# Four PSUM evictions per batch cut to one bank each in a fused recurrence and FFT-convolution kernel

## The chip, the cores and the metric

The kernel runs on one core of a Trainium2 chip. The metric is device time in microseconds; 459.4 us is the median of three runs of the kernel before (458.79 to 459.71). Engines are TensorE (PE; its weight loads are shown apart as PEld), VectorE (DVE), ScalarE (ACT), GpSimd (POOL) and SyncE (SP, which issues all transfers).

## The reference

For 4 batches of 6272 steps and 256 channels, a gated recurrence feeds a long circular convolution with two multiplicative gates:

```python
f = lower_bound + (1 - lower_bound) * sigmoid(f_logit)
h[t] = f[t] * h[t-1] + (1 - f[t]) * x[t]           # scan over 6272 steps
x1, x2, x3 = split(h @ w_proj, 3)
conv = irfft(rfft(x2, axis=1) * rfft(filter_fft, axis=0))
out = (x1 * conv * x3) @ w_out
```

## The kernel before

The DFT of length 6272 is done as 49 x 128: a first DFT over one factor, then one over the other (FT), the product with the filter's spectrum, and the two inverses. All of it is matrix products with tables that the kernel computes at the start.

The work is cut into *operations* (`op`, L80): a kind, the engines that may do it, a function that emits its instructions, and tags that it reads and writes. An operation of TensorE takes one or two of the eight PSUM banks (`take`); its result is evicted by an operation with `src` set to it. The operations are emitted in the order of a table, ORDER (L128): each entry is three characters that hold the number of the operation, its engine and its first bank. So the order on every engine, the choice between ScalarE and VectorE for each eviction (`either`, L305), and the banks are fixed by this table, and each engine works through its own list in order, waiting at semaphores.

The kinds, with the lines that the profile shows:

- **Start**: the filter is loaded, rotated (`rot`, evicted as `f2`), transformed (FF1, L661, evicted as `afs`; FF2, L679, evicted as `hw`), and its spectrum stored in DRAM and loaded back in units (Hu, Hx).
- **Recurrence of a batch** (`hgrn`): loads of x and f_logit, sigmoid on ScalarE (L337), product on GpSimd (L339), transposes on TensorE (`su`, L351), the gate f on ScalarE or VectorE (L364, L366), the scan on VectorE (L372), into HA. The recurrence of batch b+1 is worked between the steps of batch b.
- **x2 projection** (`phase_p`): 49 rows of 256 columns, two matmuls each (L725), four rows to an operation of two banks, five in the last of 12; evicted as `x2` into X.
- **First DFT** (`phase_f1`, F1, L737): 16 units of eight matmuls, two banks, evicted as `A` into HA (1024 columns). It reads all of x2.
- **Second DFT and product** (`unit`, F2, L795): the product with the spectrum is either one VectorE instruction from PSUM (L816, shown as PP) or a ScalarE copy followed by a GpSimd product (L825).
- **Inverse over q** (I2, L835): per unit 16 matmuls in two banks, evicted as `Th` (784 columns).
- **Gates** (`gate`, x13, L400): x1 and x3 per chunk, one bank each; x1 is copied out (`xs`), x3 either copied out and multiplied on GpSimd (L431), or multiplied on VectorE from PSUM (L422), into zt.
- **Output** (`phase_o`): the second inverse (I1, L869) reads all of Th; VectorE multiplies it with zt (`y`, L875); output projection (L887), four rows in two banks; evicted as `o` into one of eight places, which are then stored.

Evictions go through helpers, so ScalarE's show as L291 or L293 and VectorE's as L296 or L298, told apart by the tile that they write: X is x2, HA with 128 x 1024 is A, HA with 98 x 512 the copy ahead of a GpSimd product, Th is Th, osb, PP or HA in f32 is o, gx is a gate.

Of the kernel before, what the change touches and what calls it, by code (L numbers as in the profile page):

```python
# [21 lines left out]
S = 6272  # L22
# [26 lines left out]
NX2 = 12  # L49
# [15 lines left out]
class Plan:  # L65
# [63 lines left out]
    "AAYA+gBFgAMYABIAgVACIBBgAvWBMgAeUBTgAxSAdVBIgAkWBPgA9YANIAmUAoWA/TBGRBADBCYBogBDTBWgAtVAPIBNVAOABagBEDADgBdgBHBBhg"  # L129
    "BUTBJYBkgBOFDwgBQYBKQD8gBVDAcSArXATYAyVASIBRWDxgAVYBXAAsSApSBLIBSGBYUEIgBbSARIBZED9gEJgBeIAQAAUIBfQAFgBiVBgABpYAWY"  # L130
    "BcCEUgBlIBmQBjFAaTBnIAhXEVgBqTAZSBrDAqSAlWBwWBuSBxODyAB3UB1QBvKD+AAuWB4MBzWByYDzYB2IB+SB0GAbVB/KB6QCAUEKAB7ID0SB5Y"
    "AEYCFWD1CCBMD/YD4QCGGD2KCHUEggD5AEhgCDWCIED6IEASCEGELYCKUEBKEEWCLEECKCOQEsgEFGEtgAiUCCYCVUCJYAXYCPAEGOCXSEWAEMQCYK"
    "EQWAIAEXYAHACQSE4gEROCWEE5gCRKENAAfUAwUESOEiACTSCSYEYUCUCEOIEcWEjYFCgEdGCeSEZMFDgAKACgQEeOCfCChACZYCaSEuAEaMEkWCnQ"
    "CbCEvYElOClUE6ACoICdgAjSEmOEoQCmECjSFMgAJACiYEwUE7YEpIFNgCkCCwWB9gEqIExEE0SCxGEyMFWgCqQE1CBsYFXgC1WCrAE2KE8UFEACpY"
    "E/QBtYC2OC3SFggFAAE9MFFYCuWFhgC4CETgFBICvGAnTAGgFOACzWD7gE+MFGSCyYC0GFPYFJQFHKC+UFqgFKAFIKFrgC6WC/EC7GFQUC5YCNgFLI"
    "AYYDASFYADHWFRMFTQCMgDBCFZYFSMDIGDFSFUADQWDGCF0gDDUFVIFiAB8gDKSCcgDCYDJYDEMEnYEPgFaQDRGDLCFjYDXWFbIDVUF1gALADOSDYO"
    "DWEFcIDPCFdWDMgD3YFsADTUMTgDSYFeOFkQDUEFtYDgSFfOFlACtgFnUDhCFmIDeWFoEDaSDZYDfGErYFpMFuQF2ADbCDlWGigFvIDnUDmGF+gMfg"
    "DjSDNgF3YFwIDoEFxWC9gEbYDkCC8gJQVFyODiYDpYG0gDqQE3YJSFFzOJRTEHYDrAJVUDdgEzYJWSJTrJXEDtgF4WF7QF5GJUYEDYJYqDuUF/gF8I"
    "JaTJZYEfYDvEF6OJbSF9ICsgJfXJcLGUQJhHDsgMVAGQWGVIMggGSTGRGGGQDcgGTDGMWGHIGIUGNGJdqGCQGJEJeYGESGDIGKUGFCGOQGLEGAWGPI"
    "MhAGrgGWTGBGMUgG9gJgSGXDMrgJkRJiqMsgJlXJpQJjYJnHGYSJrIJmBGeWGZKJqUJoYGfGGaQJuVJssGbAGjWJtYGcSGnuJwFJvRGdCJzUJxpJ0Q"  # L140
    "GoYJ1EJ4XJyYJ2IGgSGsUJ6HGhKJ3YG1QGwEGluJ5XG5AHGSGkYJ7vGxYGmYJ9VHQgHHCJ+RGusJ8YGpWJ/FHMSGvYGqGG3oGtYHZgG+UG6YKABHIW"
    "HNKG4YGyQHJGHAsHKSGzAG2YHigG/YG7WKBYHLCHCsHBYKCQG8GHOTHRRHDYHrgHPLKDVHTBKEIHSYKHTMtAHVpHUYHEQKIXKJDKFtHWYKMWHFAKKv"
    "HaSKGYKOGMuYH+gH0UKLYHeqHXWH1EH4QHcqHfYHYGHjUHkYHbYH5AHnsHdYIHgH2WMiYHgSH3GHlsHoYHsQHhCH6WHuoHmYIQgHpUMWYH7GH/SHwo"
    "HvYHqEH8WKNQIBCIIUH9OHxYIZgIDqHtYIRRICYIKEHyWITBKPoIEYKRTHzGIMsKQYKSUIiQIAYKTDIsgILYIFWIjAINYKUsKWTIVpKVYKXVIGGMXQ"
    "KZFIJYI1gKYLIUYIWYIaWMYAMbUIeGMZIIOSM3gMcEKbXISYIPCMdMIbYIXQKaYKdHImSIYAIcuMegMjUM4gInCIkQMkMIdYIfYIoWIlAKcTMlMKgS"
    "JHgIpGItQKerKiCIqUMnWIvoKfYIxAKhTNDgMoGIyYIgRIrMNEgIwYM5AMpOI+gKlQI2UIhBKjrMvWIuYKnAM6YI6sKkYMzSMwGKmQNQgI4EMxOKqR"
    "I7YNPgM0CIzUKsBI5YM1KM7WI0ENFAKrVKooKvSKttKpYM8GM/QJAYI3YKuYNGYKxCJIUM9ONbgNAAI8SNcgJMEMqgNBIKwWJKEK0XI9CI/UKyuK2H"
    "K1QJDsKzYJLYK5WK3ANHSNRAJBsK4YNLQNICNmgK7ONSYJEYJCYJFUNlgNMANJKK6WJGEK+XNdANNIK/VNTTJJYLAHNeYK8uNXQNUDLBtK9YLDXNvg"
    "NYANVLLEWLCYNwgLFHLISLJVLKCLNXLGuLLFNfSNZILHYJNYLPHNiVNgCLOXN6gNnANhKLMYN5gJOQNjFNoYLQvRtTJPANkNLRYRuXRvDLSQRwHLXS"
    "LTINxANpUNsWLYKNqENyYLUQODgNtGOEgNrMLZSLVANuOLcUMaYLaCLWgNzQLdMRyXN0ALhSR0HN1IN2UN7ALmWONgN3ELiKOOgLeQN8YLbgOFAN4M"  # L150
# [24 lines left out]
    "ZjEbZYZrubaRZZYaBgbbSdkgbfQbdCZpuZsYZaUbcBbhAd5SbeYZbMZqYZkQZwWeVgd6CZlIeWgaCUZ0Gd7KZoYUqgbgQZxYaGEZ1YUlgbkXaEEblR"
    "ZyubiAZtUbmHZ5SZzYZuEbnpbjYeBWZ7qboYZ9CeFQeCGZ+YbpUeggdsAZ8YZ2SeDObrEbqVZ3CbuUeEgbstbvWZ6YeGAaHYefgbwMbzXbtYeXAeNS"
    "eHIb0Vb1Hb4UbxueOCeIgaFYZ/Qb2tbyYb6Eb5WePKb3YaAAeRUb9XepgaDYeSEb7ueYYaIQeqgb/HeTMb8Yb+WaJAcCXcDTcAucEHcHVUtQcFreUY"
    "cBYcJFcISUuId8YehAcGYcMWcKqeZQcLYcNOecUeiYeaAinSezgedEebIioTe0gcOWiqDeeMipCcRQcPGejScSIcWUcQgekCemWerAcXMA2Qe9gcTQ"
    "e+genGesYelKcYUcUAeoOcbScZEcVgcgQUvgccKetWe1AewUchIcdSe2YfHgexEfIgeuGeyMcagAzRceCclQevOe/AA0Vd4Ye3Ue6ScmIfAYe4EciW"
    "fSge7CfRge5McnQcjGe8KcqUcoAA1XcvWcrMfJAfBQfEScwOfCAfKYisVfFCitUfDIcsWivEiuFfGKc0QeQYctGfLUdgYc1IcugcxSfMEfTAfNMfUY"  # L180
    "c5QcyCfOWc6IczgfVUfPGc2ScfgfWEckgfQOc7Qc3CfXMfYWc4gdDUfZOc8Ac+SfaOdEMfdWftQc/KfeGffUfuIfnSfgEfbWfoKfvQfcOfjUfwAdAS"
    "fkEfhWdBCfrQfiGdCgcpgfxSfsAdIWfyCfpQdJOirYflVfqAixTiwYfmFiyUizLi2Xi0EdKQfzSi4HdLIi1Yf1Uf0Cf3Qf2Mf5Wf4Af9Si3Uf6GgBq"
    "A3Ri7Vi5EgFWf/qgCYi9Ff7QgNTi6YgJGi8Vf8IgAYgngjAXi+tf+YjBSgGYjCHgKYgDQi/YgPDjDqjFXgEAgRrjEYgVSjGVgQYgXCgHujKQgSYjHH"
    "gdRjMAjLUjItgIYgwggeBgLWjNsjJYgOYg5gjPQgMGgZqjOYgYYgfUjQRggEgjWjRIgaYghSjSBjUUgWYhCggkOgiCjVVgTQjWEjXNglSgoWgUAgmK"
# [12 lines left out]
def kernel(  # L197
# [72 lines left out]
    def At(u):  # L270

        return [("At", u % NA)]
# [438 lines left out]
    def phase_p(b):  # L711
        hn = [("hn", kh, c) for kh in range(2) for c in range(NCHK)]
        for g in range(NX2):
# [4 lines left out]
            def rows(pb, nb=nb):  # L718
                return PS[:, pb:pb + nb].rearrange("m a (r e) -> m (a r) e", e=256)
# [258 lines left out]
```

## Time and profile before

| | before |
|---|---|
| median of three runs | 459.4 us |
| span of the profiled execution | 458.7 us |
| instructions | 14602 |
| busy: PE, DVE, ACT, POOL | 444.4, 406.4, 400.5, 301.9 us |
| granted TensorE clock | 1.000 |
| HBM over the span | 257 GB/s |

The page gives the profiled execution by its span, from the first to the last instruction; the 0.7 us to the median of the runs lie around it or are the difference between executions. Busy times are the union of an engine's records. A record of ScalarE or VectorE ends when its last write is through, which overlaps the start of the next one by about a tenth of a microsecond; a matmul's end is modelled. In a line of a timeline the first number is the start, the second the length, and "xN" says that N instructions were merged into it; in brackets stands the idle time ahead of it and what ended it. In a line of groups the numbers after the bar are busy time and the mean of one in ns. In a line of waits: total, times, longest.

### The profile page before, as it was taken

Reading aid. Unit: us, or ns where it says so; the run is one execution under the profiler, and the core shown is the slowest. Engines: PE = TensorE matmul, PEld = TensorE weight load, DVE = VectorE, ACT = ScalarE, POOL = GpSimd, SP = SyncE. Lnnn points to the kernel's source line nnn. Section 1 sums busy time; section 2 is a strip of 40 time slices with the busy share of each in tenths; the row PEclk is TensorE's granted clock in tenths of the full one; section 3 lists DMA queues with packets and bytes.
Section 4 is the critical chain, followed back from the end, with each engine's and each line's share of the span. In section 5 each row is a group of like instructions: output and inputs, shape, how many; then the busy total and the mean of one; then the engine's idle time right before and its main releaser. Section 6 shows DMA issues by size and latency. Waiting matters only on the chain.

```text
span 458.7 us, 14602 instructions
## 1 busy us (share of the span) xinstructions
PE 444.4 (97%) x6009; PEld 346.8 (76%) x6009; DVE 406.4 (89%) x459; ACT 400.5 (87%) x551; POOL 301.9 (66%) x279
## 2 busy tenths in 40 slices
PE   8998999999999999999999999999999999999996
PEld 6777777867766889777668879767768798777785
DVE  8389998699999997999999986999999984999974
ACT  4899998999999988989998969999999869889563
POOL 5377993179899742988996525979896503878500
PEclk9999999999999999999999999999999999999999
DMA  8998999957898898368869897388789542576077
GB/s 321 384 374 300 339 402 372 334 149 210 253 334 273 287 302 325 122 195 298 289 236 317 311 309 298 139 300 282 232 318 307 188 186 93 184 227 201 34 285 292
DMA packets 45298, 121.53 MB, mean 265 GB/s; under 512 B 4400, under 2 KB 8496, under 8 KB 45232
## 3 DMA queue, kind: packets, MB, share of 16 engines
q1 hardware_dynamic: 45232, 120.60, 74.8%
q8 instruction: 47, 0.77, 0.7%
q14 instruction: 19, 0.16, 0.1%
HBM read 86.12 MB, written 31.98 MB: 257 GB/s over the span
## 4 chain that ended last, share of the span: by engine, by line
PE 64%; DVE 12%; ACT 8%; DMA 7%; issue 5%; POOL 2%; SPq 1%; DVEq 0%; ACTq 0%; POOLq 0%
PE PS L400 15%; PE PS L725 9%; PE PS L835 9%; PE PS L351 6%; PE PS L887 6%; PE PS L795 6%; PE PS L737 6%; DVE HA L372 5%; DMA X<-in_moe_filter_fft_dram 4%; DVE ys L875 3%; PE PS L661 3%; DMA XT<-in_x_dram 2%; PE PS L869 2%; ACT fTs L364 2%; DMA out_dram<-PP 2%
## 5 line engine op out<-in xcount | busy, mean ns | idle before, releaser
L339 POOL TENSOR_TENSOR XT<-XT,FL 128x1024 f32<-128x1024 f32 (+1 forms) x49 | 109.7, 2243 | 53.9 <-ACT FL L337 47.3
L372 DVE TENSOR_TENSOR_SCAN HA<-fTs,HA,PS 128x512 f16<-128x512 f32 (+1 forms) x96 | 113.2, 1204 | 1.8 <-ACT fTs L364 1.0
L400 PE MATMUL PS<-HA,W 128*128 128x490 f16 (+1 forms) x416 | 102.9, 368 | 1.7 <-issue 0.7
L825 POOL TENSOR_TENSOR PP<-HA,Hu 98x1008 f16<-98x1008 f16 x40 | 83.9, 2104 | 8.0 <-ACT HA L291 3.9
L291 ACT CAST HA<-PS 128x1024 f16<-128x1024 f32 (+1 forms) x98 | 79.1, 834 | 5.3 <-PE PS L737 2.7
L431 POOL TENSOR_TENSOR zt<-gx 128x490 f16<-128x490 f32 (+1 forms) x37 | 44.9, 1219 | 43.0 <-issue 15.6
L875 DVE TENSOR_TENSOR ys<-PS,zt 128x1024 fp32r<-128x1024 f32 (+1 forms) x52 | 58.7, 1152 | 10.0 <-PE PS L869 7.0
L816 DVE TENSOR_TENSOR PP<-PS,Hu 98x1008 f16<-98x1008 f32 x56 | 65.8, 1202 | 0.9 <-issue 0.5
L364 ACT ACTIVATE fTs<-PS,cc 128x512 f32<-128x512 f32 (+1 forms) x85 | 56.1, 675 | 5.8 <-PE PS L351 4.8
L887 PE MATMUL PS<-Wo,ys 128*128 128x256 f32 x392 | 58.1, 294 | 1.6 <-DVE ys L875 1.3
L400 PEld LDWEIGHTS <-W 128*128 128x128 f16 x416 | 34.8, 97 | 31.6 <-issue 8.1
L835 PEld LDWEIGHTS <-PP 98*128 98x128 f16 x1024 | 50.0, 97 | 10.8 <-issue 1.8
L835 PE MATMUL PS<-VV,PP 98*128 98x98 f16 x1024 | 55.9, 206 | 0.7 <-DVE PP L816 0.5
L887 PEld LDWEIGHTS PS<-Wo,ys 128*128 128x128 f32 x392 | 49.8, 189 | 6.4 <-DVE ys L875 1.4
L291 ACT CAST Th<-PS 128x784 f16<-128x784 f32 x59 | 48.3, 821 | 5.7 <-PE PS L835 5.2
L293 ACT ACTIVATE gx<-PS 128x490 f32<-128x490 f32 (+1 forms) x86 | 49.7, 585 | 2.4 <-PE PS L400 1.0
L337 ACT ACTIVATE FL<-FL 128x1024 f32<-128x1024 f32 (+1 forms) x49 | 49.2, 1009 | 0.0
L422 DVE TENSOR_TENSOR zt<-PS,gx 128x490 f16<-128x490 f32 (+1 forms) x67 | 42.8, 650 | 2.7 <-PE PS L400 1.2
L725 PE MATMUL PS<-W,HA 128*128 128x256 f16 x392 | 44.6, 273 | 0.2
L725 PEld LDWEIGHTS <-HA 128*128 128x128 f16 x392 | 43.0, 142 | 1.2 <-issue 0.2
L351 PE MATMUL PS<-iden,FL 64*128 64x64 f32 x736 | 41.9, 230 | 1.1 <-DVE Hx L296 0.5
L351 PEld LDWEIGHTS PS<-iden,FL 64*128 64x128 f32 x736 | 31.3, 138 | 14.3 <-DVE HA L372 2.6
(129 smaller groups left out, 738.6 us busy)
## 6 DMA issues: line engine op xcount, KB each, us to landing
FL<-in_f_logit_dram SPq DMA_DIRECT2D x45, 512.0 KB, 5.6
XT<-in_x_dram SPq DMA_DIRECT2D x45, 512.0 KB, 6.2
Hu<-H SPq DMA_DIRECT2D x39, 512.0 KB, 4.7
out_dram<-osb SPq DMA_DIRECT2D x22, 512.0 KB, 4.4
out_dram<-PP SPq DMA_DIRECT2D x16, 512.0 KB, 5.2
Hx<-H SPq DMA_DIRECT2D x13, 512.0 KB, 4.5
out_dram<-HA SPq DMA_DIRECT2D x10, 512.0 KB, 4.9
X<-in_moe_filter_fft_dram SPq DMA_DIRECT2D x9, 512.0 KB, 7.3
```

The source lines that it names most:

```text
L291: nc.scalar.copy(dst, src)
L339: op("u", {"POOL": 0.1 + 0.553 * nb}, lambda e, xt=xt, ft=ft: nc.gpsimd.tensor_tensor(xt, xt, ft, op=AOP.mult), r=[("ft", k)], w=[("xt", k)])
L351: nc.tensor.transpose(bank(pb)[:, at[p] + j:at[p] + hn:nb], src[ps, j, cols], iden[ps, ps])
L364: nc.scalar.activation(fT, sT, AF.Identity, scale=by, bias=1.0)
L372: nc.vector.tensor_tensor_scan(h, fT, bank(pb)[:, 512 - hn:512 + hn], init, op0=AOP.mult, op1=AOP.add),
L400: nc.tensor.matmul(PS[:, p, 0:n], W13[:, kh, js], HA[:, HB[kh] + t0:HB[kh] + t0 + n], start=(kh == 0), stop=(kh == 1))
L725: nc.tensor.matmul(pp[:, r - r0, :], column(HB[kh], q_of(r)), W2[:, kh, :], start=(kh == 0), stop=(kh == 1))
L816: nc.vector.tensor_tensor(pr, px.unsqueeze(1).broadcast_to([TB, 2, UE, 63]), hh, op=AOP.mult)
L825: nc.gpsimd.tensor_tensor(pr, spec[:, o, :, 1:64].unsqueeze(1).broadcast_to([TB, 2, UE, 63]), hh, op=AOP.mult)
L835: nc.tensor.matmul(PS[:, ib + o, pr * TB:(pr + 1) * TB], PP[:TB, k, o, n, 2 * pr:2 * pr + 2, :], v[:TB], start=(n == 0), stop=(n == 1))
L875: nc.vector.tensor_tensor(late["ys"][:, yk, :, 0:rn * 128], PS[:, cb:cb + 2, 0:rn * 128], late["zt"][:].rearrange("p k r m -> p k (r m)") ...
L887: nc.tensor.matmul(po[:, i, :], late["ys"][:, yk, kh, i * 128:(i + 1) * 128], Wo[:, kh, :], start=(kh == 0), stop=(kh == 1))
```

## The change

The operations P (x2 projection), F1, I2 and proj are cut into operations of one PSUM bank, each with its own eviction. P becomes 25 operations of two rows (the last of one), NX2 goes from 12 to 25. F1 becomes two operations of four matmuls per unit, with a tag At per half. I2 becomes one operation per half spectrum o, so it waits for the products of that half alone. The output projection becomes one operation for two rows; the store still waits for both halves, and is as large as before. The second inverse I1, `y`, F2, the gates and the recurrence keep their operations. The matmuls are the same in number and shape.

The order table is new as a whole: 2866 operations instead of 2410. On ScalarE there are 737 instead of 548, on VectorE 468 instead of 426. Evictions on ScalarE and VectorE: x2 30 and 18 before, 56 and 44 after; A 55 and 9, then 113 and 15; Th 59 and 5, then 111 and 17; o 49 and 3, then 96 and 4. Gate f on ScalarE and VectorE: 85 and 19, then 88 and 16. The x3 gates done as one VectorE product: 67, then 78. Spectrum products on VectorE: 83, then 84.

```diff
-NX2 = 12
+NX2 = 25
...
-        return [("At", u % NA)]
+        return [("At", u % NA, o) for o in range(2)]
...
+            r0 = 2 * g
+            rn = min(2, Q - r0)
...
-            pp = op("P", {"PE": 0.005 + 0.214 * rn}, mm, r=hn + Wr(0) + Wr(1) + ["W2"], take=nb)
+            pp = op("P", {"PE": 0.005 + 0.214 * rn}, mm, r=hn + Wr(0) + Wr(1) + ["W2"], take=1)
...
-        f1 = op("F1", {"PE": 0.056 * UE}, mm, r=[("x2", g) for g in range(NX2)] + ["D1"], take=2)
...
-        op("A", either(1024), lambda e, pb: copy(
...
+        for h in range(2):
...
+            f1 = op("F1", {"PE": 0.028 * UE}, mm, r=[("x2", g) for g in range(NX2)] + ["D1"], take=1)
+            op("A", either(512), lambda e, pb, k=k + h * UE // 2: copy(
...
-        i2 = op("I2", {"PE": 0.695}, inv,
-                r=[("P", k, 0), ("P", k, 1), ("Pz", k, 0), ("Pz", k, 1), "VA", "VB"], take=2)
-        op("Th", either(784), lambda e, ib: copy(
...
+            i2 = op("I2", {"PE": 0.3475}, inv, r=[("P", k, o), ("Pz", k, o), "VA", "VB"], take=1)
+            op("Th", either(392), lambda e, ib, o=o: copy(
...
-            po = op("proj", {"PE": 0.259 * rn}, proj, r=[("y", yk)], take=2)
...
-            op("o", either(256 * rn), lambda e, ob, place=place, rn=rn: copy(
...
+            for h in range((rn + 1) // 2):
+                hn = min(2, rn - 2 * h)
...
+                po = op("proj", {"PE": 0.259 * hn}, proj, r=[("y", yk)], take=1)
+                op("o", either(256 * hn), lambda e, ob, place=place, h=h, hn=hn: copy(
```

More of the change, by code (lines that the diff above doesn't have):

```diff
@@ L134 @@
[L134 to L138, printed above, removed]
@@ L189 @@
[L189 to L192 removed]
+    "AAYABIAMYACIANIAOAAtRAjXAsWBFgAPIAdXAZWAxWArRAbWAiVBTgBBgA+gBIgBMgBPgA9YBCYATYAVYASIAUIARIBGSAqUBUUAgWA/WAmQBDQBag"
@@ L487, in prepare @@
         op("W", {"ACT": 0.5}, lambda e: act.copy(Wo[:], wo[:]), r=[("W", 0, 0)], w=["Wo"])
-        scr, st = HA[:, A0:A0 + AW], [("At", i) for i in range(NA)]
+        scr, st = HA[:, A0:A0 + AW], [t for i in range(NA) for t in At(i)]
         ti = scr[:, 0:2004].bitcast(I32)
@@ L713, in phase_p, with mm @@
         for g in range(NX2):
-            r0 = 4 * g
-            rn = Q - r0 if g == NX2 - 1 else 4
-            nb = (rn + 1) // 2
-            def rows(pb, nb=nb):
-                return PS[:, pb:pb + nb].rearrange("m a (r e) -> m (a r) e", e=256)
-            def mm(e, pb, r0=r0, rn=rn, rows=rows):
-                pp = rows(pb)
-                for r in range(r0, r0 + rn):
+            r0 = 2 * g
+            rn = min(2, Q - r0)
+            def mm(e, pb, r0=r0, rn=rn):
+                for i in range(rn):
@@ L724, in mm @@
                     for kh in range(2):
-                        nc.tensor.matmul(pp[:, r - r0, :], column(HB[kh], q_of(r)), W2[:, kh, :],
+                        nc.tensor.matmul(PS[:, pb, 256 * i:256 * i + 256], column(HB[kh], q_of(r0 + i)), W2[:, kh, :],
                                          start=(kh == 0), stop=(kh == 1))
-            pp = op("P", {"PE": 0.005 + 0.214 * rn}, mm, r=hn + Wr(0) + Wr(1) + ["W2"], take=nb)
-            op("x2", either(256 * rn), lambda e, pb, r0=r0, rn=rn, rows=rows: copy(
+            pp = op("P", {"PE": 0.005 + 0.214 * rn}, mm, r=hn + Wr(0) + Wr(1) + ["W2"], take=1)
@@ L729, in phase_p @@
+            op("x2", either(256 * rn), lambda e, pb, r0=r0, rn=rn: copy(
                 e, both(xv[:, :, r0:r0 + rn]),
-                rows(pb)[:, 0:rn, :].rearrange("m r (i e) -> m i e r", e=2)), w=[("x2", g)], src=pp)
+                PS[:, pb, 0:256 * rn].rearrange("m (r i e) -> m i e r", r=rn, e=2)), w=[("x2", g)], src=pp)
     def phase_f1(b, u):
-        def mm(e, pb):
-            pa = PS[:, pb:pb + 2].rearrange("m a (i c) -> m (a i) c", c=128)
-            for i in range(UE):
-                j = (u * UE + i) * PW
-                nc.tensor.matmul(pa[:, i, :], X2[:, j:j + 128], D1[:], start=True, stop=True)
@@ L738, in phase_f1, with mm @@
-        f1 = op("F1", {"PE": 0.056 * UE}, mm, r=[("x2", g) for g in range(NX2)] + ["D1"], take=2)
-        k = u % NA * UE
-        op("A", either(1024), lambda e, pb: copy(
-            e, A[:, k:k + UE],
-            PS[:, pb:pb + 2].rearrange("p a (i r k) -> p (a i) r k", r=2, k=64)),
-           w=At(u) + Ax(u), src=f1)
+        k = u % NA * UE
+        for h in range(2):
+            def mm(e, pb, h=h):
+                for i in range(UE // 2):
+                    j = (u * UE + h * UE // 2 + i) * PW
+                    nc.tensor.matmul(PS[:, pb, 128 * i:128 * i + 128], X2[:, j:j + 128], D1[:], start=True, stop=True)
+            f1 = op("F1", {"PE": 0.028 * UE}, mm, r=[("x2", g) for g in range(NX2)] + ["D1"], take=1)
+            op("A", either(512), lambda e, pb, k=k + h * UE // 2: copy(
+                e, A[:, k:k + UE // 2],
+                PS[:, pb].rearrange("p (i r k) -> p i r k", r=2, k=64)),
+               w=[At(u)[h], Ax(u)[h]], src=f1)
@@ L871, in inv @@
                                              start=(rr == 0), stop=(rr == 1))
-            i1 = op("I1", {"PE": 0.115 * rn}, inv, r=[("Th", u) for u in range(NU)] + ["ID"], take=2)
+            i1 = op("I1", {"PE": 0.115 * rn}, inv, r=[("Th", u, o) for u in range(NU) for o in range(2)] + ["ID"], take=2)
             yk = g % 2
```

172 lines of the change are left out of this document (94 added, 78 removed).

## The prediction

> **What bounds the kernel now.** I read the page's busy shares first, then busy time by stretches that I cut around the projection of x2, then the waits of VectorE, then the timelines at the cuts.
>
> ```profile
> span 458.7 us, 14602 instructions
> PE 444.4 (97%) x6009; PEld 346.8 (76%) x6009; DVE 406.4 (89%) x459; ACT 400.5 (87%) x551; POOL 301.9 (66%) x279
> ```
>
> TensorE at 97% looks like the bound. But a matmul's record contains the time in which it drains, so short pauses between groups of matmuls vanish in it. The stretches say more.
>
> ```profile
> core 0: us, PE busy (x) PEld busy (x) DVE busy (x) ACT busy (x) POOL busy (x), PEclk, DMA share, GB/s
> 0.00:30.00 30.00, 27.63 (x171) 21.59 (x173) 18.73 (x51) 21.88 (x23) 15.27 (x35) 1.00 0.94 365
> 30.00:75.50 45.50, 43.57 (x566) 33.43 (x565) 44.29 (x48) 44.30 (x65) 38.10 (x43) 1.00 0.96 345
> 75.50:91.00 15.50, 15.49 (x149) 13.49 (x148) 8.99 (x11) 13.65 (x17) 1.23 (x1) 1.00 0.97 359
> 91.00:171.00 80.00, 77.48 (x1221) 58.10 (x1218) 78.69 (x83) 75.12 (x110) 64.94 (x52) 1.00 0.80 257
> 171.00:187.00 16.00, 16.00 (x170) 15.08 (x169) 12.56 (x12) 12.45 (x14) 6.60 (x3) 1.00 0.73 291
> 187.00:272.00 85.00, 83.81 (x1279) 63.14 (x1278) 82.85 (x87) 78.20 (x116) 65.70 (x54) 1.00 0.78 259
> 272.00:287.00 15.00, 14.93 (x148) 14.16 (x147) 9.84 (x10) 13.38 (x14) 6.52 (x4) 1.00 0.77 310
> 287.00:371.00 84.00, 82.28 (x1276) 61.88 (x1275) 82.03 (x87) 77.29 (x115) 65.00 (x53) 1.00 0.74 253
> 371.00:386.00 15.00, 15.00 (x147) 13.94 (x142) 7.42 (x9) 11.69 (x14) 3.10 (x3) 1.00 0.37 143
> 386.00:430.00 44.00, 43.98 (x582) 31.02 (x580) 41.92 (x50) 38.40 (x57) 33.63 (x34) 1.00 0.51 160
> 430.00:458.70 28.70, 24.25 (x338) 20.96 (x334) 19.07 (x19) 14.14 (x15) 1.78 (x2) 1.00 0.61 244
> ```
>
> There are two kinds of stretch. In four **turns** (75.5 to 91, 171 to 187, 272 to 287, 371 to 386: 61.5 us) TensorE is full and VectorE idles 22.7 us. In the **middles** (91 to 171, 187 to 272, 287 to 371, 386 to 430: 293 us) VectorE idles only 7.5 us, ScalarE 24.0. So the middles last as long as VectorE's work, with ScalarE close behind; the turns as long as TensorE's.
>
> **What a split costs.** Every matmul stays as it is; the evictions of x2, A, Th and o are cut in two. A record's tail overlaps its successor, so the price of an instruction is the spacing in a chain: the chain's length less one record, divided by the others.
>
> ```profile
> 186.94 1.93 ACT L291 CAST HA<-PS 128x1024 f16<-128x1024 f32 x2
> 206.26 1.52 ACT L291 CAST Th<-PS 128x784 f16<-128x784 f32 x2
> 210.58 1.57 ACT L291 CAST HA<-PS 98x512 f16<-98x512 f32 x3
> 280.16 3.49 DVE L296 CAST X<-PS 128x1024 f16<-128x1024 f32 x3 [0.45 <-PE PS L725]
> 62.48 0.68 DVE L296 CAST Hx<-PS 128x512 fp32r<-128x512 f32 x1
> 63.08 1.27 DVE L372 TENSOR_TENSOR_SCAN HA<-fTs,HA,PS 128x512 f16<-128x512 f32 x1
> ```
>
> ```profile
> L291 ACT CAST HA<-PS 128x1024 f16<-128x1024 f32 x55 | 55.1, 1025 | 3.9 <-PE PS L737 2.7 <-POOL PP L825 0.5 <-issue 0.2
> L291 ACT CAST HA<-PS 98x512 f16<-98x512 f32 x43 | 24.0, 590 | 1.3 <-PE PS L795 0.9
> L296 DVE CAST X<-PS 128x1024 f16<-128x1024 f32 x18 | 21.6, 1222 | 11.8 <-PE PS L725 11.8
> L296 DVE CAST Th<-PS 128x784 f16<-128x784 f32 x5 | 4.9, 970 | 0.0
> ```
>
> ScalarE: 1024 columns 0.91 us (1.93 - 1.02), 784 about 0.70, 512 0.49 ((1.57 - 0.59) / 2). VectorE: 1024 1.13, 512 0.60 (63.08 - 62.48), 784 0.88 (its 0.97 less the 0.09 by which 1.22 exceeds 1.13). Either way a split costs 0.07. For 392 columns, which before does not have, I take half of 784 and half that cost: 0.39 and 0.47 (bounds 0.35 and 0.49, 0.44 and 0.60).
>
> [...]
>
> **Where they go.** The new order is a table, so I counted operations in both tables, inside each turn (first to last projection of x2) and outside. Durations not yet shown:
>
> ```profile
> L366 DVE TENSOR_SCALAR fTs<-PS,cc 128x512 f32<-128x512 f32 x15 | 11.1, 743 | 1.0 <-PE PS L351 0.3
> L422 DVE TENSOR_TENSOR zt<-PS,gx 128x490 f16<-128x490 f32 x61 | 39.5, 659 | 2.3 <-PE PS L400 1.2 <-ACT gx L293 0.6
> L875 DVE TENSOR_TENSOR ys<-PS,zt 128x1024 fp32r<-128x1024 f32 x48 | 57.0, 1213 | 5.1 <-PE PS L887 2.3 <-PE PS L869 2.2 <-ACT gx L291 0.2
> L364 ACT ACTIVATE fTs<-PS,cc 128x512 f32<-128x512 f32 x81 | 54.9, 691 | 5.0 <-PE PS L351 4.1 <-DVE HA L372 0.3
> L400 PE MATMUL PS<-HA,W 128*128 128x490 f16 x384 | 96.9, 371 | 1.7 <-issue 0.7 <-DVE HA L372 0.4 <-ACT Th L291 0.2
> L887 PE MATMUL PS<-Wo,ys 128*128 128x256 f32 x392 | 58.1, 294 | 1.6 <-DVE ys L875 1.3
> ```
>
> 1. *VectorE inside the turns: +11.0 us, at no time of its own.* x2 there goes from 16 whole evictions to 42 pieces (+6.4), gate products (xs as a product) from 1 to 5 (+2.3 at 0.57), a gate copy (+0.6), a y (+1.1), an o half (+0.6). They lie beside TensorE's matmuls, in 22.7 us of idle VectorE. Were that cover gone, they would cost up to 11.0.
> 2. *TensorE inside the turns: +3.1 us, paid.* Five gate projections of two matmuls move into the first turn (5 x 2 x 0.25, the row's 96.9 by 384), and three half output projections stand where one whole was (0.6 more, at 0.148 a matmul). The same work leaves the middles, where VectorE was the later one, so nothing comes back for it.
> 3. *VectorE outside the turns: -5.5 us, gained.* A: 15 halves for 9 wholes, -1.2. Th: 17 halves for 5, +3.6. x2 left over behind the cut, 2 halves for 2 wholes, -1.1. Gates f: 16 for 19 at 0.66, -2.0. xs: 12 copies fewer and 7 products more at 0.57, -2.9. One y fewer, -1.1. Products with the spectrum: two copies fewer, one product more, -0.1. In the start, three half evictions of the filter's DFT fewer, one of its spectrum more, -0.7. Three more evictions of f2 (+3.4) fall into the first 30 us, where VectorE is busy 18.73, and cost nothing; if the start is late already, they cost up to 3.4.
> 4. *ScalarE outside the turns: +7.4 us, of which I charge 2.* A: 113 halves for 55 wholes, +5.3; Th: 111 for 59, +1.4; o: 91 for 48, +1.4; three more f at 0.6, +1.8; fewer left over x2, -3.0; small ones +0.5. That goes into 24.0 us of idle ScalarE beside VectorE. But an engine that goes from 92% to about 94% also makes others wait more often. Nothing before shows how often, so the bounds are 0 and 7.4, and I take a value near the lower end since the nearest rows, the middles, show VectorE without a wait.
> 5. *The turnover: -3 us.* F1 needs all of x2, and nothing can be multiplied until the first F1 and A have followed. The last steps now:
>
> ```profile
> 175.96 1.59 ACT L291 CAST X<-PS 128x1280 f16<-128x1280 f32 x1 [0.87 <-PE PS L725]
> 186.28 0.62 PE L737 MATMUL PS<-D,X 128*128 128x128 f16 x8
> 379.47 5.31 ACT L291 CAST X<-PS 128x1024 f16<-128x1024 f32 x5
> 381.69 0.43 DVE L875 TENSOR_TENSOR ys<-PS,zt 128x256 fp32r<-128x256 f32 x1 [4.41 <-PE PS L869]
> 384.03 0.67 DVE L298 TENSOR_SCALAR gx<-PS 128x490 f32<-128x490 f32 x1 [1.91 <-PE PS L400]
> ```
>
> An eviction of x2 (1.59, elsewhere 1.02), an F1 (0.62) and an A (1.02) become some 0.6, 0.3 and 0.6: about 1.5 us less in each turn, 6 in all. In the fourth turn ScalarE evicts five x2 in a row while VectorE stands still for 4.41 and 1.91 us; in the new table they alternate more. Some of this time was filled with gate work already, so I take half: -3, bounds 0 and -6.
>
> ```profile
> 75.53 10.70 PE PS L725 x98
> ```
>
> The added handovers I cost at nothing: TensorE's operations go from 770 to 998, but in this row of the chain of work 98 matmuls of twelve operations run at 0.109 us each, their eleven handovers included. GpSimd gets 11 gate products fewer. SP's and POOL's queues carry the same transfers, loads in nearly the same order; a late load in the first 30 us (DMA share 0.94) would cost its lateness in full, and I have no row for that.
>
> Sum on the span: 458.7 + 3.1 - 5.5 + 2.0 - 3.0 = 455.3. The runs shown have a median of 459.4, 0.7 above this span, so the forecast is **456.0**.
>
> **The rivals.** *ScalarE takes over the middles (slower).* Its idle there comes in waits for TensorE that cannot be moved, and each extra start delays an operand that VectorE or TensorE needs next. Then the +7.4 are paid whole and the turnover gives nothing: 458.7 + 3.1 - 5.5 + 7.4 = 463.7, with the 0.7, 464.4. For it: ScalarE is at 92% in the middles. Against it: VectorE's idle of 7.5 us there. It decides where VectorE begins to wait for evictions of A and Th, say 12 us or more in the middles. [...]
>
> *The turns open fully (much faster).* All 6 us of item 5 come, and nothing is lost to ScalarE: 458.7 + 3.1 - 5.5 - 6.0 = 450.3, as a time 451.0. For it speaks this row, in which VectorE waits a dozen times for half a microsecond of projection more than a one-bank eviction would need:
>
> ```profile
> DVE X L296 <- PE PS L725: 11.8, 12, 3.0
> ```
>
> Against it: TensorE is full there and sets the turns' length anyway.
>
> *No difference.* The -5.5 of item 3 is mostly moved work that the tail (430 to 458.7, VectorE 19.07 of 28.7) had room for, item 5 halves again: within 1 us of 459.4.
>
> **How the numbers follow.** Forecast (452 to 458.4) 0.42; turns open fully 0.12; no difference 0.10; ScalarE takes over 0.28, and a dearer form of it, with late loads besides, 0.08. Sums of the bounds: 451.0, with half a microsecond less if 392 columns take VectorE 0.44, and, with items 4 and 5 at their worst and the f2 evictions paid, 467.8. The range 450 to 466 leaves out about 0.18; since both signs hold much, the forecast's own range stands beside it. A measurement of this kernel tells 0.2%, 0.9 us, from no change: faster 0.54, same 0.10, slower 0.36.
>
> **What would show it.** Item 1 and 3: VectorE busy in the turns up by about 11 us, in the middles down by some 5 with idle still near 7.5. Item 2: the first turn longer by 2 us, the others not. Item 4: ScalarE's busy time near 410 us (+7.4 here, +2.7 in the turns, -0.7 in the start); if VectorE waits for A, Th or gates in the middles, the rival is right. Item 5: the first product with the spectrum follows the last x2 matmul about 1 us sooner. Wrong would be a chain spacing of 512 columns above 0.55 on ScalarE, or a start (to the first x2 matmul, 75.5 now) that is over 2 us later.

## The result, and the profile after

The changed kernel takes 456.52 us (median of four runs, 456.24 to 456.89) against 459.55 for the kernel before, measured beside it: a ratio of 0.993, 95% interval 0.9909 to 0.995. It is faster by some 3 us; 456.0 was forecast. The sum was near, but several of its terms were not, and they missed in opposite directions; the reason given for the largest term is not shown.

The page of the changed kernel (span, busy times):

```profile
span 454.8 us, 14864 instructions
PE 442.5 (97%) x6009; PEld 346.2 (76%) x6009; DVE 416.3 (92%) x501; ACT 404.9 (89%) x739; POOL 286.3 (63%) x266
```

The two profiled spans differ by 3.9 us, the medians by 3.0; so the ledger below, made of spans, overstates the gain by a microsecond. Next the busy time by stretch. This time I cut each turn exactly, from its first x2 matmul to the first product with the spectrum. First the kernel before, then the changed kernel:

```profile
0.00:75.36 75.36, 71.06 (x731) 54.88 (x732) 62.88 (x99) 66.04 (x86) 53.38 (x77) 1.00 0.95 353
75.36:90.90 15.54, 15.53 (x147) 13.53 (x146) 9.03 (x11) 13.69 (x17) 1.23 (x1) 1.00 0.97 358
90.90:171.00 80.10, 77.58 (x1223) 58.20 (x1220) 78.80 (x83) 75.22 (x111) 64.94 (x52) 1.00 0.80 257
171.00:186.40 15.40, 15.40 (x162) 14.59 (x161) 11.96 (x12) 11.99 (x13) 6.00 (x3) 1.00 0.75 302
186.40:271.50 85.10, 83.92 (x1282) 63.21 (x1281) 82.95 (x88) 78.66 (x117) 66.30 (x54) 1.00 0.77 258
271.50:288.50 17.00, 16.92 (x178) 15.91 (x179) 11.64 (x12) 14.69 (x15) 8.02 (x4) 1.00 0.70 279
288.50:371.20 82.70, 80.98 (x1254) 60.65 (x1249) 80.93 (x86) 76.17 (x114) 63.50 (x53) 1.00 0.75 258
371.20:387.40 16.20, 16.20 (x160) 14.89 (x160) 8.44 (x9) 12.89 (x16) 3.65 (x3) 1.00 0.32 126
387.40:458.67 71.27, 66.83 (x892) 50.93 (x890) 59.76 (x67) 51.14 (x71) 34.86 (x34) 1.00 0.56 197
```

```profile
0.00:72.95 72.95, 69.45 (x728) 53.95 (x728) 63.36 (x97) 63.40 (x88) 52.99 (x76) 1.00 0.93 336
72.95:90.30 17.35, 16.84 (x153) 14.34 (x152) 13.60 (x23) 14.55 (x25) 0.00 (x0) 1.00 1.04 401
90.30:168.60 78.30, 77.00 (x1219) 57.93 (x1217) 77.35 (x82) 75.09 (x145) 63.71 (x50) 1.00 0.82 272
168.60:184.60 16.00, 15.65 (x168) 14.86 (x167) 13.89 (x19) 14.01 (x24) 4.79 (x2) 1.00 0.71 268
184.60:268.10 83.50, 82.69 (x1279) 62.67 (x1276) 82.11 (x89) 79.98 (x156) 63.75 (x51) 1.00 0.78 265
268.10:285.60 17.50, 17.07 (x176) 15.74 (x174) 13.83 (x22) 15.39 (x26) 9.04 (x5) 1.00 0.75 279
285.60:367.10 81.50, 80.90 (x1255) 61.39 (x1252) 79.10 (x86) 77.72 (x152) 62.34 (x53) 1.00 0.75 262
367.10:383.70 16.60, 16.05 (x159) 14.67 (x159) 12.11 (x19) 12.75 (x23) 2.44 (x2) 1.00 0.36 142
383.70:454.77 71.07, 66.82 (x894) 50.64 (x891) 60.92 (x74) 52.03 (x106) 27.24 (x28) 1.00 0.53 190
```

The reader is to go down the two lists in pairs. The columns are those of the prediction's list of stretches: length, then busy time of PE, PEld, DVE, ACT, POOL. The start is 2.4 us shorter. The four turns are longer, 67.5 us in sum for 64.1, and VectorE is busy 53.4 us in them instead of 41.1. The three middles are shorter by 1.8, 1.6 and 1.2, in sum 4.6, with 4.1 us less of VectorE's work and 2.7 more of ScalarE's. The tail is the same. So the whole gain that is left after the trade of start and turns comes out of the middles. One profile's sum carries about a microsecond of its own, however: two kernels of the table below that cannot be told from the one before, split_a_th and split_o, have middles of 246.7 and 246.5 where its profile has 247.9. The gain in the middles is therefore 3.3 to 4.6 us.

### The profile page after: what moved, and what is told of

It reads as the page before. It is cut to its first block, busy times and chain, and to the rows that moved or that the text cites. A ratio compares the mean times of both kernels' runs of the same rounds, so it can differ in the third digit from the quotient of the medians.

```text
span 454.8 us, 14864 instructions
## 1 busy us (share of the span) xinstructions
PE 442.5 (97%) x6009; PEld 346.2 (76%) x6009; DVE 416.3 (92%) x501; ACT 404.9 (89%) x739; POOL 286.3 (63%) x266
## 4 chain that ended last, share of the span: by engine, by line
PE 73%; DVE 7%; DMA 7%; POOL 5%; ACT 5%; issue 3%; DVEq 0%; POOLq 0%; ACTq 0%
PE PS L412 17%; PE PS L911 10%; PE PS L842 10%; PE PS L363 8%; PE PS L745 7%; PE PS L732 7%; PE PS L802 6%; PE PS L875 4%; DVE HA L384 3%; POOL XT L351 3%; DMA XT<-in_x_dram 2%; PE PS L673 2%; DMA HA<-in_moe_filter_fft_dram 2%; ACT X L303 2%; DVE ys L881 1%
## 5 line engine op out<-in xcount | busy, mean ns | idle before, releaser
L412 PE MATMUL PS<-HA,W 128*128 128x490 f16 (+1 forms) x416 | 113.8, 367 | 0.6 <-ACT gx L305 0.3
L303 ACT CAST HA<-PS 128x512 f16<-128x512 f32 (+1 forms) x157 | 91.6, 642 | 6.3 <-PE PS L802 4.4
L842 PEld LDWEIGHTS <-PP 98*128 98x128 f16 x1024 | 54.2, 97 | 19.0 <-issue 2.5
L443 POOL TENSOR_TENSOR zt<-gx 128x490 f16<-128x490 f32 (+1 forms) x26 | 31.5, 1216 | 54.1 <-ACT gx L303 33.1
L376 ACT ACTIVATE fTs<-PS,cc 128x512 f32<-128x512 f32 (+1 forms) x88 | 60.5, 709 | 5.0 <-PE PS L363 3.4
L842 PE MATMUL PS<-VV,PP 98*128 98x98 f16 x1024 | 63.3, 206 | 0.1
L305 ACT ACTIVATE gx<-PS 128x490 f32<-128x490 f32 (+1 forms) x91 | 57.0, 631 | 3.6 <-PE PS L412 2.7
L303 ACT CAST Th<-PS 128x392 f16<-128x392 f32 x111 | 56.4, 554 | 1.4 <-PE PS L842 1.2
L434 DVE TENSOR_TENSOR zt<-PS,gx 128x490 f16<-128x490 f32 (+1 forms) x78 | 50.2, 651 | 4.7 <-PE PS L412 3.1
L745 PE MATMUL PS<-D,X 128*128 128x128 f16 x512 | 42.6, 219 | 0.1
```

The lines of the kernel that those rows point to most:

```text
L303: nc.scalar.copy(dst, src)
L412: nc.tensor.matmul(PS[:, p, 0:n], W13[:, kh, js], HA[:, HB[kh] + t0:HB[kh] + t0 + n], start=(kh == 0), stop=(kh == 1))
L745: nc.tensor.matmul(PS[:, pb, 128 * i:128 * i + 128], X2[:, j:j + 128], D1[:], start=True, stop=True)
L842: nc.tensor.matmul(PS[:, ib, pr * TB:(pr + 1) * TB], PP[:TB, k, o, n, 2 * pr:2 * pr + 2, :], v[:TB], start=(n == 0), stop=(n == 1))
```

## The experiments

All times are compared as ratios to the kernel before, measured beside each. The table has the medians, the ratios with their 95% intervals, and the same four sums of stretches, cut in each profile in the same way (us; from unrounded times, so that a tenth may differ from the rows above). Where the text takes the difference of two medians, they are of different sessions; by the ratios such a difference comes out up to 0.7 us otherwise, with an interval of some 1.1 us to either side for two kernels set against each other.

| kernel | median | ratio to before | start | turns | middles | tail |
|---|---|---|---|---|---|---|
| before | 459.55 | 1 | 75.4 | 64.2 | 247.9 | 71.2 |
| changed | 456.52 | 0.993 (0.9909 to 0.995) | 73.0 | 67.5 | 243.2 | 71.1 |
| split_all | 461.23 | 1.0041 (1.0027 to 1.0054) | 75.2 | 66.1 | 247.3 | 70.9 |
| split_x2 | 462.06 | 1.0058 (1.0044 to 1.0073) | 75.4 | 66.1 | 247.4 | 71.8 |
| split_a_th | 460.01 | 1.0005 (0.9996 to 1.0014) | 75.1 | 64.4 | 246.7 | 71.1 |
| split_o | 459.09 | 0.9992 (0.9979 to 1.0004) | 75.8 | 64.1 | 246.5 | 71.1 |
| before_relief | 461.82 | 1.0039 (1.0023 to 1.0056) | 75.3 | 65.3 | 247.6 | 71.4 |
| dve_dose | 459.32 | 0.9986 (0.9974 to 0.9999) | 72.5 | 67.4 | 246.5 | 71.5 |
| act_dose | 460.40 | 0.9999 (0.9986 to 1.0011) | 72.6 | 67.4 | 247.5 | 71.3 |
| after_relief | 464.41 | 1.0092 (1.0071 to 1.0114) | 72.6 | 68.9 | 248.2 | 72.8 |
| act_light | 456.52 | 0.9933 (0.9912 to 0.9954) | 72.6 | 67.5 | 243.4 | 70.8 |
| dve_light | 455.91 | 0.9917 (0.9899 to 0.9935) | 72.6 | 66.5 | 243.9 | 70.7 |
| pe_light | 456.57 | 0.9923 (0.9907 to 0.9939) | 72.7 | 67.4 | 244.3 | 70.2 |
| x2_back | 469.32 | 1.0197 (1.0171 to 1.0224) | 72.7 | 79.3 | 244.9 | 70.4 |

### The pieces without the new order

*split_all* has the code of the change, word for word but for the table. The table is the old one with each entry of P, x2, F1, A, I2, Th, proj and o written as its halves:

```diff
-(P g, PE, bank p) ... (x2 g, engine e, bank p)
+(P 2g, PE, p) (P 2g+1, PE, p+1) ... (x2 2g, e, p) (x2 2g+1, e, p+1)
```

> The kernel before with its own order and its own choice of engines; every operation of P, F1, I2 and proj is cut in two (the code of the change), the halves standing one behind the other at the old place, in the two banks that the whole had. Theory (the order makes the gain: VectorE's work moved out of the middles; a split by itself only costs 0.07 us on its engine, 158 to 193 of them on ScalarE, some 35 on VectorE): 460 to 463 us. Rival (the smaller pieces make the gain, since banks and operands are free sooner): 456 to 457.5 us.

It came out at 461.23: the pieces alone cost 0.4%, and the changed kernel, with the same instructions on the tensor engine and the same pieces, is 4.7 us faster than it (5.1 by the ratios). With these pieces the order makes the gain; the pieces by themselves lose. A new order with whole evictions was not tried, so whether the gain needs the pieces at all is open. The other three split one kind, or two, in the same way.

> The kernel before with P and x2 alone cut in two, in place. Theory of the forecast's turnover step: the last eviction of x2 ends some 1 us sooner in each turn, half of it useful: 457.5 to 459. Rival (the turn is set by TensorE and by the order behind it): within 0.5 us of before, the first product with the spectrum as late after the last x2 matmul as before (4.0 to 5.8 us).

The turnover theory fell, and its rival too: 462.06, slower by 0.6%. The timeline of ScalarE and that of VectorE in the fourth turn of split_x2 show why:

```profile
379.77 6.51 ACT L294 CAST X<-PS 128x512 f16<-128x512 f32 x11
382.00 0.43 DVE L873 TENSOR_TENSOR ys<-PS,zt 128x256 fp32r<-128x256 f32 x1 [4.70 <-ACT X L294]
```

The run of five whole evictions that took 5.31 us in the kernel before takes 6.51 us as eleven pieces, and VectorE stands behind it, for longer than its 4.41 us before. The rows of the changed kernel by shape give the price:

```profile
L303 ACT CAST X<-PS 128x512 f16<-128x512 f32 x54 | 32.5, 689 | 7.6 <-PE PS L732 5.8 <-DVE ys L881 1.6
L308 DVE CAST X<-PS 128x512 f16<-128x512 f32 x42 | 27.2, 692 | 7.5 <-PE PS L732 7.2
L303 ACT CAST X<-PS 128x256 f16<-128x256 f32 x2 | 2.7, 1370 | 0.0
L308 DVE CAST X<-PS 128x256 f16<-128x256 f32 x2 | 2.7, 1328 | 0.0
```

The piece of one row, 256 columns, takes 1.37 or 1.33 us, twice as long as two rows. I had put a last piece at 0.6 from contiguous copies. In split_x2 the one-row piece stands last in the first turn and runs until 2.33 us after the last x2 matmul, where the whole eviction ended at 1.61; in the fourth it is the 21st of 25, within the run of eleven shown above.

> The kernel before with F1 and A, I2 and Th alone cut in two, in place: 114 more evictions on ScalarE and 14 on VectorE, all in the middles. Theory (VectorE sets the middles, its 14 splits cost 1 us; ScalarE's 8 us go into its idle 24 us): 459.5 to 461. Rival (finer pieces help the middles): 457 to 458.5. Second rival (ScalarE sets the middles): 464 or more.

460.01, a ratio whose interval contains 1: 114 splits on ScalarE and 14 on VectorE cost nothing that can be told. That fits the theory's range; its explanation was not yet tested.

> The kernel before with proj and o alone cut in two, in place: 45 more evictions on ScalarE, 3 on VectorE. Theory: ScalarE's 3 us lie beside VectorE's y and scans: 459 to 460.5. Rival (the half projections let o and the next y start sooner): 457.5 to 458.5.

459.09, again no difference that can be told. Of the four kinds only x2 loses by its pieces.

### Who takes the evictions of x2

```diff
-(x2, DVE) for 44 of 100 pieces in the changed kernel's table
+(x2, DVE) for 22 of them, (x2, ACT) for every second one
```

> The changed kernel with every second of VectorE's 44 evictions of x2 given to ScalarE, in place: 22 x 0.6 = 13 us less on VectorE, 22 x 0.5 = 11 us more on ScalarE, all in the turns, where ScalarE idles 10.8 us in sum. Theory (VectorE's share of x2 lies in its idle time at no cost, and keeps ScalarE from setting the turns): the turns longer by 4 to 9 us in sum, 460 to 465, the middles as before. Rival (the turns are as long as TensorE's matmuls, whoever evicts): within 1.5 us, 455 to 458.

469.32, 12.8 us slower than the changed kernel, beyond what I expected. It is the clearest result of the study. The third turn of x2_back, and TensorE's costliest wait of the whole run (in sum, times, longest):

```profile
273.94:296.92 22.98, 18.98 (x177) 16.70 (x174) 10.30 (x16) 18.54 (x32) 8.99 (x5) 0.93 0.56 208
```

```profile
PE PS L732 <- ACT X L303: 8.8, 10, 1.7
```

The turn is 5.5 us longer than the changed kernel's; VectorE idles 12.7 us in it, and TensorE stops its projection for ScalarE's evictions, 4.0 us of the 8.8 in this turn. The granted clock was 0.93 here (see the last section), but the other three turns, all at 1.00, are 6.3 us longer in sum too. The middles lose only 1.7 us. So in the turns VectorE's share of x2 is what keeps TensorE going.

### More work on one engine, then less

The doses add starts of instructions without adding columns:

```diff
+# dve_dose: each of 84 spectrum products as two of half the columns
+for i in range(0, UE, UE // 2): ... px[:, s], pr[:, :, s], hh[:, :, s]
+# act_dose: 85 of ScalarE's A evictions as two of 256 columns
+m = UE // 4 if e == "ACT" and u % 4 else UE // 2
```

> The changed kernel with each of VectorE's 84 products with the spectrum done as two instructions of half the columns: some 84 x 0.07 = 5.9 us more of VectorE's work, nearly all in the middles. Theory (the middles last as long as VectorE's work): 4.5 to 6.5 us slower than the changed kernel, 461 to 463. Rival (VectorE is one of several that share the middles, and its extra work hides beside the others): 0 to 3 us slower.

> The changed kernel with the A evictions of ScalarE in three units of four done as two instructions of 256 columns: some 85 more, at 0.07 each 5.9 us of ScalarE's work in the middles, the same dose as for VectorE. Theory (ScalarE lies beside VectorE, its idle time takes the dose): 0 to 2 us slower than the changed kernel, 456.5 to 458.5. Rival (ScalarE has become a bound of the middles): 4 us or more slower, 460.5 or more.

In chains a half product has a spacing of 0.590 us for 1.115 whole, so the whole dose on VectorE was 84 x 0.065 = 5.5 us; it cost 2.8 us (2.6 by the ratios). A piece of 256 columns has 0.264 for 0.478, so the dose on ScalarE was 4.25 us; it cost 3.9 (3.2). Taken so, VectorE's work seems paid by half and ScalarE's nearly in full. But the doses did not lie where the expectations had them, nearly all in the middles. The three middles of dve_dose, then those of act_dose:

```profile
89.87:168.72 78.85, 77.38 (x1219) 57.97 (x1217) 78.22 (x103) 75.27 (x146) 63.72 (x50) 1.00 0.81 272
184.66:270.23 85.57, 83.62 (x1278) 63.18 (x1278) 83.31 (x110) 80.23 (x157) 63.80 (x51) 1.00 0.77 260
287.71:369.79 82.08, 81.14 (x1257) 61.51 (x1252) 79.96 (x107) 77.91 (x152) 62.43 (x53) 1.00 0.76 260
```

```profile
89.95:169.63 79.68, 77.91 (x1218) 58.38 (x1217) 77.64 (x82) 76.52 (x166) 63.91 (x50) 1.00 0.84 269
185.57:270.85 85.28, 83.40 (x1278) 63.05 (x1278) 82.49 (x90) 80.87 (x175) 63.76 (x51) 1.00 0.78 261
288.36:370.95 82.59, 82.02 (x1257) 61.72 (x1252) 79.34 (x86) 79.07 (x170) 62.38 (x53) 1.00 0.76 258
```

Of the 84 split products 62 lie in the three middles and 22 in the tail. In the middles VectorE got 62 x 0.065 = 4.0 us more, and they became 3.3 us longer (246.5 for 243.2); the tail, with 1.4 us more, became 0.4 longer. Of ScalarE's 85 pieces 54 lie in the middles: 54 x 0.05 = 2.7 us more by the spacing, 3.7 us by busy time, and they became 4.3 us longer (247.5), while VectorE's idle time in them rose from 4.7 to 8.1 us. So in the middles additions to either engine are paid nearly in full or in full, with about a microsecond of uncertainty in each sum. That ScalarE lies beside VectorE at no cost, as the theory of act_dose had it, has fallen; by its median, 460.40, its rival (460.5 or more) was just missed too. For dve_dose the rival's range (0 to 3 us) held, but not its reason: what cost little was the part of the dose that lay in the tail.

The busy time of the two engines rose with their doses, VectorE's by 3.9 us and ScalarE's by 4.4 (first the row of dve_dose, then that of act_dose):

```profile
PE 444.6 (97%) x6009; PEld 347.7 (76%) x6009; DVE 420.2 (92%) x585; ACT 405.6 (89%) x739; POOL 286.5 (63%) x266
```

```profile
PE 445.3 (97%) x6009; PEld 347.6 (76%) x6009; DVE 417.1 (91%) x501; ACT 409.3 (89%) x824; POOL 286.6 (62%) x266
```

That is 0.046 us for each of 84 starts on VectorE and 0.052 for each of 85 on ScalarE.

The reliefs move gate copies from VectorE to ScalarE, in place, by the engine in the table alone (13 in the changed kernel, 12 in the kernel before).

> The changed kernel with VectorE's 13 gate copies given to ScalarE, nothing else moved: 7.5 us less on VectorE (13 x 0.575), 6.1 us more on ScalarE (13 x 0.47). Theory (VectorE alone sets the middles): up to 7 us faster than the changed kernel, 449.5 to 453. Rival (both are full): no faster, 456 to 460, with VectorE then waiting for ScalarE's evictions.

> The kernel before with 12 of VectorE's 24 gate copies given to ScalarE, nothing split and nothing else moved: 6.9 us less on VectorE, 5.6 us more on ScalarE. Theory (moving VectorE's work out of the middles is what gains, with operations of any size): 453.5 to 457.5. Rival (it takes the smaller operations to do so): 459 or more.

464.41 and 461.82: both slower, the first by 7.9 us, more than the 6.1 us that ScalarE was given. VectorE's work fell to 408.8 us and its idle time in the middles rose from 4.7 to 11.8. One line of VectorE's waits in after_relief says what it stood for:

```profile
DVE zt L434 <- ACT gx L305: 10.6, 10, 2.2
```

In the changed kernel this line is 0.9 us in three waits (in before_relief 3.5, before 0.6). VectorE's gate products waited for the copies that ScalarE now made late in its own list. So the reliefs do not show what less work on VectorE is worth: they put a wait in its place. They were also smaller than I had written, for the middles: of the 13 copies only 4 stand there, 6 in the turns and 3 in the tail, and VectorE's busy time in the middles fell by 2.2 us. What the two runs show is that giving VectorE's copies to ScalarE gains nothing in either kernel.

I then took work away without moving anything. In act_light and dve_light some gate copies leave out 420 of their 490 columns, in pe_light 15 gate projections do; what depends on those columns is not computed.

```diff
-copy(e, xs(1), px)
+copy(e, xs(1)[:, s1], px[:, s1])     # s1: 7 of 49 rows for the copies chosen
...
-                    def mm(e, p, js=js, t0=t0, n=n):
+                    mn = n // 7 if len(plan.ops) in SHORT else n
```

> The changed kernel in which every eighth of ScalarE's 117 gate copies (15) copies 70 of its 490 columns, the rest of the columns being left out: some 15 x 0.35 = 5.2 us less on ScalarE, no instruction moved or dropped. New theory (since 4.25 us more on ScalarE cost some 3.5 and 5.5 us more on VectorE some 2.7, both set the middles together, ScalarE rather more): 2 to 4 us faster than the changed kernel, 452.5 to 454.5. Rival (the order is so tuned that any change of a length costs, less work as well as more): no faster, 456 or more. The forecast's theory (ScalarE lies beside VectorE): within 1 us, 455.5 to 457.5.

> The changed kernel in which VectorE's 13 gate copies copy 70 of 490 columns each, the rest left out: some 13 x 0.45 = 5.9 us less on VectorE. New theory (both set the middles together): 1.5 to 3.5 us faster than the changed kernel, 453 to 455. Forecast's theory (the middles last as long as VectorE's work): 4.5 to 6 us faster, 450.5 to 452. Rival (ScalarE alone is the bound now): within 1 us, 455.5 to 457.5.

> The changed kernel in which 15 of TensorE's 208 gate projections, spread over the four batches, multiply 70 of their 490 columns, the rest left out: 15 x 2 x 0.175 = 5.2 us less on TensorE, nothing moved or dropped; the same dose as was taken from ScalarE and from VectorE, where it gained 0 and 0.6 us. New theory (in the changed kernel TensorE's list has become the longest in the middles, the others wait for it): 3 to 5 us faster than the changed kernel, 451.5 to 453.5. Rival (the three lists are tied so that less work on one alone brings nothing): within 1 us, 455.5 to 457.5.

456.52, 455.91 and 456.57: the same as the changed kernel, within the intervals. The work did go; the busy rows of act_light, dve_light and pe_light, to be held against the changed kernel's ACT 404.9 and DVE 416.3:

```profile
PE 441.6 (97%) x6009; PEld 346.2 (76%) x6009; DVE 416.6 (92%) x501; ACT 401.1 (88%) x739; POOL 286.1 (63%) x266
```

```profile
PE 442.3 (98%) x6009; PEld 346.3 (76%) x6009; DVE 411.5 (91%) x501; ACT 404.5 (89%) x739; POOL 286.4 (63%) x266
```

```profile
PE 441.0 (97%) x6009; PEld 346.1 (76%) x6009; DVE 415.9 (91%) x501; ACT 404.8 (89%) x739; POOL 286.6 (63%) x266
```

ScalarE's busy time fell by 3.8 us and VectorE's by 4.8. For TensorE the row can't show it, since its records overlap: from the start of one matmul to the next, the shortened ones took 0.036 us (median), the others 0.207, with records of 0.37. But again only a part lies in the middles. Of ScalarE's 15 copies 11 do, and its busy time there fell by 2.5 us; of TensorE's 30 shortened matmuls 20 do, some 3.4 us; of VectorE's 13 copies only 4 do, and its busy time there fell by 1.3 us (237.3 for 238.6):

```profile
89.20:168.05 78.85, 77.38 (x1221) 58.18 (x1219) 76.98 (x82) 75.45 (x148) 63.84 (x50) 1.00 0.82 274
184.11:267.63 83.52, 82.72 (x1279) 62.59 (x1276) 81.43 (x89) 79.69 (x156) 63.70 (x51) 1.00 0.79 266
284.92:366.45 81.53, 80.94 (x1256) 61.32 (x1251) 78.85 (x86) 77.89 (x152) 62.53 (x53) 1.00 0.76 261
```

So a saving of 2.5 us on ScalarE alone or of some 3.4 on TensorE alone in the middles brings nothing, where additions of that size to ScalarE or VectorE cost. For VectorE the test was too small: 1.3 us paid in full would lie inside the interval of dve_light (0.6 us faster, some 1.2 to either side), so it does not decide against the forecast's theory, which had assumed all 5.9 us in the middles. That three lists are tied to each other by their waits, an addition to one making the others late and a saving on one being spent waiting, fits all of this, but is argued and not shown. A larger saving on VectorE in the middles, or a saving on two or three engines at once, was not tried. Neither was GpSimd, which idles 53 us in the three middles, nor the transfers (DMA share 0.75 to 0.82 there). In all three runs the theory named first had expected a gain.

## Why the prediction was right, point by point, and where it was not

*VectorE's work in the turns (+11.0 at no time of its own).* Nearly right: its busy time there rose by 12.4 us, and TensorE waited for VectorE twice in the turns, 0.8 us in sum. What happens if ScalarE has to do half of these pieces showed in x2_back: the turns grew by 11.8 us.

*TensorE in the turns (+3.1, paid, "nothing comes back for it").* The turns became 3.3 us longer, but that is the sum of three things. First the first turn's x2 projection, before and changed; then the third turn from the last x2 matmul to the first product, before and changed:

```profile
75.36:86.23 10.87, 10.87 (x100) 10.79 (x99) 5.87 (x6) 9.26 (x11) 0.00 (x0) 1.00 0.96 345
72.95:86.72 13.77, 13.26 (x110) 11.94 (x109) 10.24 (x17) 11.71 (x19) 0.00 (x0) 1.00 1.04 400
282.75:288.55 5.80, 5.79 (x82) 5.04 (x83) 4.44 (x7) 5.58 (x6) 5.80 (x4) 1.00 0.13 51
279.59:285.56 5.97, 5.97 (x76) 4.81 (x75) 4.96 (x10) 5.16 (x11) 4.41 (x4) 1.00 0.24 93
```

Over the four turns the x2 projections are 4.5 us longer (50.1 for 45.6): 2.7 of it is TensorE's work, for which 3.1 was forecast, and 1.8 is waiting. Behind the last x2 matmul 1.2 us came off. That nothing comes back for the work was only in part right: of the ten gate matmuls more in the first projection four came from the start, four from behind the projection in the same turn, and two out of a middle. The sign to look for was a first turn 2 us longer and the others not; they are 1.8 and, for the other three, 0.4 to 0.6 longer.

*VectorE outside the turns (-5.5).* The size was near: 4.1 us less work in the middles, middles 3.3 to 4.6 us shorter. The reason, "the middles last as long as VectorE's work", is not shown. The dose on VectorE fits it (4.0 us more, 3.3 longer), dve_light was too small to tell, and after_relief put a wait in place of the work. But VectorE is not alone: act_dose made the middles 4.3 us longer without any work for VectorE. The agreement of the two sizes is therefore no proof that the one made the other. What is shown: the new order, with the pieces, is worth 4.7 us over the same pieces in the old order. Which of its moves in the middles are worth how much is open; to split the new table into its moves wasn't tried.

*ScalarE outside the turns (+7.4, of which 2 charged).* ScalarE's busy time went up by 4.4 us, not by 10: 3.4 in the turns, 3.6 in the middles and the tail, and 2.6 less in the start. A split of A or Th was priced too high: in split_a_th 114 more evictions raised ScalarE's busy time by 4.5 us, 0.04 each for the 0.07 of the sum. In the three middles its idle time sank from 17.9 to 10.5 us. That the rest is not free, as the rival had it, act_dose showed. In the changed kernel itself the rival did not come about.

*The turnover (-3).* This is the step that failed. The sentence was that the last eviction of x2, the F1 and the A "become some 0.6, 0.3 and 0.6: about 1.5 us less in each turn", half of it useful. Between the last x2 matmul and the first product lay 4.65, 4.19, 5.80 and 3.96 us; in the changed kernel 3.58, 4.07, 5.97 and 3.79. That is 0.3 us less on average, 1.2 in sum for the 3 forecast. The pieces did what was expected of them: the last x2 eviction, in each turn one of two rows, ends 0.5 us sooner on average, and so does the first F1 start (0.72, 0.96, 1.09 and 0.92 us after the last x2 matmul, for 1.67, 1.44, 1.18 and 1.35). But TensorE's records leave no gap from the last x2 matmul to the first product in either kernel (busy 18.58 of 18.60 us in the four turns before, 17.41 of 17.41 changed; an x2 matmul's record of 0.27 us reaches 0.16 us past the next start, 0.109 us behind its own, so a pause shorter than that would not show). Output projections, gates and further F1 stand in its list ahead of the F2 that the product needs; in the third turn that F2 starts 4.87 us after the last x2 matmul before, 4.89 changed. So the sooner F1 was filled with other work, all of it and not the half that was assumed, and the 1.07 us of the first turn are about the four gate matmuls (4 x 0.25) that had been put ahead. "TensorE is full there and sets the turns' length anyway", the prediction's own argument against its second rival, was the right one. With the old order it was worse: split_x2 made two of the four longer, to 5.37 and 5.15, by the one-row piece and because a split of x2 costs more on ScalarE than the 0.07 of contiguous ones: 0.53 of spacing twice, for 0.91.

*The handovers at nothing.* Not right in the turns. In the kernel before TensorE waits nowhere in the x2 projections (the prediction's row of 98 matmuls in 10.70 us). In the changed kernel it waits once in each:

```profile
PE PS L732 <- ACT X L303: 1.0, 2, 0.5
PE PS L732 <- DVE gx L310: 0.5, 1, 0.5
PE PS L732 <- DVE X L308: 0.3, 1, 0.3
```

That is 1.8 us for a term that was put at nothing. Elsewhere nothing speaks against it: split_a_th and split_o add 161 evictions on ScalarE and no time that can be told.

So it was luck that the forecast came out close. On the span -3.4 was forecast and -3.9 measured: the turns came out 3.2 us worse than forecast (+3.3 for +0.1), the start 1.7 better (-2.4, where -0.7 was in the sum), and the middles up to 1.8 better (-4.6 for -2.8, the charge for ScalarE included). The start is shorter in every kernel with the new order (72.5 to 73.0 us for 75.1 to 75.8); the four gate matmuls that left it are some 1.0 us, and what made the rest is open.

## What to carry to other kernels

Where three engines are each some 90% busy in an in-order schedule, don't take the busiest one for "the bound": test by taking work away as well as by adding it, since here an addition cost (2.8 us for the dose on VectorE, 3.9 for that on ScalarE) and a saving on ScalarE or TensorE brought nothing (456.52 and 456.57 us for 456.52). Count first how much of the dose lies in the stretch that the theory is about; of VectorE's 13 gate copies only 4 did. A sooner operand gains little where the engine that needs it has other work in its list until then: here the first F1 started 0.5 us sooner on average, the first product came 0.3 us sooner. Splitting evictions was no gain by itself here; a new order for the smaller pieces was, and half of VectorE's x2 evictions in it can't be given to ScalarE without a loss of 12 us (x2_back). Price a split with the layout that it will write: a short piece can be the dearest, as the 256 columns at 1.37 us were here beside the 512 at 0.69.

## What the runs showed of the hardware that I had not expected

The eviction of one row of x2 (256 columns into single f16 elements that lie apart) took 1.37 us on ScalarE and 1.33 on VectorE, that of two rows (512 columns, pairs of elements) 0.69 on both, and four rows (1024) 1.02 and 1.22 before. Both engines slow down alike; whether the write to single elements is the cause was not tried by itself.

On ScalarE a mean record grew from 590 ns to 631 for the 98 x 512 copies, with the same spacing in chains (0.48): the records of the two kernels cannot be compared by their means.

In the third turn of x2_back the granted clock was 0.93, and 1.00 in every stretch of the changed kernel. Three cuts in that turn show where:

```profile
279.01:282.42 3.41, 1.20 (x10) 0.94 (x9) 0.00 (x0) 2.77 (x5) 0.00 (x0) 1.00 1.02 414
282.42:285.83 3.41, 3.33 (x16) 2.60 (x16) 1.29 (x2) 3.41 (x7) 0.00 (x0) 0.50 1.03 422
285.83:289.25 3.42, 2.81 (x26) 2.65 (x24) 1.29 (x2) 1.79 (x4) 2.39 (x1) 1.00 0.19 75
```

The clock was halved for one stretch of 3.41 us, right behind 3.41 us in which TensorE was busy for 1.20, with waits of 1.71 and 0.58 us for ScalarE. Up to half of that stretch, 1.7 us of the turn's 5.5, may be the clock's: an estimate from the 3.41 us and the 0.50. What made the clock fall is not shown by these rows.
